# Queries loaded two groups at a time, two tokens on a partition, and put in order by copies of their transposes

## The chip, the cores and the metric

The kernel runs on one core of one Trainium2 chip. The metric is the device time of one execution in microseconds (us). One profiled execution gives the trace that is read here. In it, PE is the matrix engine (PEld its weight loads), DVE, ACT and POOL are the vector, scalar and GpSimd engines, and SP only issues transfers. "L224" is line 224 of the kernel as listed.

## The reference, cut to what matters

The input is four batches of 8 heads, 768 tokens and 64 features. Lightning attention works on blocks of 64 tokens, with a state that decays from block to block; its output, 512 wide for a token, goes through a mixture of depths, in which 128 tokens of each batch, those with the highest gate score, pass an expert of two matrices.

```
for b in range(768 // 64):
    intra = (q_b @ k_b.T * Dmask) @ v_b          # Dmask: lam ** (i - j), zero above the diagonal
    inter = (q_b * lam_pow) @ kv_state
    out[b] = intra + inter
    kv_state = lam_block * kv_state + (k_b * rev_pow).T @ v_b
x = out, heads side by side                      # (4, 768, 512)
scores = x @ w_gate
top = the 128 tokens of a batch with the highest scores
out[top] = x[top] + sigmoid(scores[top]) * (relu(x[top] @ w1) @ w2)
```

## The kernel before

**Groups.** A group is 128 tokens (two blocks) of one batch with all 8 heads, so there are 24 groups, six a batch (`NT`). The main loop runs over `g` from 0 to 23. Step g finishes group g, makes the scores of group g+1, and prepares group g+2: its transposes, decayed queries and state products. The order of all instructions on each engine is the order of the program; the kernel writes it out by hand. Each engine works through its instructions in that order, and an instruction that waits holds up those behind it.

**Loads.** `load(g)` fetches queries, keys and values of a group as three DMAs of 256 KB from the SP queue, each a tile of 128 partitions (tokens) by 8 heads by 64 features. One head of one token is contiguous in memory: 256 bytes, one packet. In `fetch_in` (L67) a load waits for the one three before it, except in a stretch in which the weights are loaded, so that about three are under way. The main loop asks for loads three to five groups ahead.

**Transposes.** Scores need queries and keys with features on the partitions. For groups under `SPLIT` (16), `transposes(g)` makes four PE transposes of queries (L219; each takes two heads, 128 x 128) into the PSUM tile `tq`, and ACT copies `tq` to its part of `qkT` in SBUF in one instruction (L224). Then come four of keys (L233) into `tk` and their copy (one copy, L238, up to group 7; two, L243, after that, because the keys' transposes then lie in the banks of the state products `pu`). From group 16 on `split_transposes` does it in another way (L257, with copies L263 to L265).

**What follows.** POOL multiplies keys and queries by their decay (`kd` L205, `qs` L270) and the states (`decayed` L318). PE makes the state products (`pu` L308), scores (L285), the part from states (L345) and the part from scores (L356); DVE masks the scores (`p` L292) and adds the states (L335, or L330). ACT copies outputs to `x_b` (L370, L372), from which DVE takes the gate scores (`xg` L395). A row of scores is turned by PE (`pb` L418), copied by ACT (`sc_row` L421), and compared by DVE (L424, L434).

**PSUM banks.** `tq`, `tk`, `tqk`, `pb`, `pk` and the expert's tiles share two PSUM banks in turn (`bank`); while the expert holds one (`hold=True`, tiles `ph` and `py`), all others take turns in the one left.

**Experts.** `plan(b)` spreads the expert of batch b over later steps. Work is put at a step with a key, and `in_order` runs what stands at one step by rising keys; the expert's 16 pieces have keys 10, 20, 30. `ranks` and `tokens` find the chosen tokens: PE counts in `pk` (L486), and DVE turns this into indices (`tok_f` L492, `tok` L495), with which POOL gathers rows (`fetch`, L509).

Of the kernel before, what the change touches and what calls it, by code (L numbers as in the profile page):

```python
# [8 lines left out]
FP32 = mybir.dt.float32  # L9
# [8 lines left out]
def kernel(  # L18
# [12 lines left out]
    nc = tc.nc  # L31

    B, H, S, D = q.shape
    HD = H * D
    F = moe_w1.shape[1]
    CAP = moe_capacity
    L = 128
    C = 64
    NT = S // L
    NHP = H // 2  # L40
# [5 lines left out]
    SPLIT = 2 * NT + 4  # L46
    FED = 2 * NT
    half = [slice(0, C), slice(C, 2 * C)]
    assert D == 64 and H % 2 == 0 and S % L == 0 and HD == 512 and F % 512 == 0
    assert 0 <= CAP < S  # L50

    const = ctx.enter_context(tc.tile_pool(name="const", bufs=1))
    ld = ctx.enter_context(tc.tile_pool(name="ld", bufs=7))
# [8 lines left out]
    loaded, issued = {}, []  # L62

    def fetch_in(out, in_):


        dma = nc.sync.dma_start(out=out, in_=in_)  # L67
        n, n_w1, n_w2 = len(issued), F // 256, NFC * HD // 512
        if 3 <= n < 3 * (NT + 3) + n_w1 or n >= 3 * (FED + 1) + n_w1 + n_w2:
            tc.add_manual_dep(  # L70
                dma.ins, issued[-3].ins.name,
                mybir.DependencyInfo(mybir.DependencyClass.Sync, mybir.DependencyReason.DATA),
                reason="loads under way",
            )
        issued.append(dma)

    def load(g):
        b, c = divmod(g, NT)
        rows = slice(c * L, (c + 1) * L)
        tiles = []  # L80
        for name, src in (("qn", q), ("kn", k), ("vn", v)):
            t = ld.tile([128, H, D], FP32, name=name)
            fetch_in(t[:], src[b, :, rows, :].rearrange("h p d -> p h d"))
            tiles.append(t)
        loaded[g] = tiles
# [14 lines left out]
    def load_weights(i):  # L100
# [13 lines left out]
    ident = const.tile([128, 128], FP32, name="ident")  # L114
# [10 lines left out]
        out=not_before[:], in_=not_before[:], compare_op=ALU.is_ge, fill=0.0,  # L125
# [58 lines left out]
    def bank(shape, name, hold=False):  # L184

        tag = next(t for t in banks if t not in held)
        banks.remove(tag)
        banks.append(tag)
        if hold:
            held.append(tag)  # L190
        return ps_m.tile(shape, FP32, name=name, tag=tag)
# [20 lines left out]
    def transposes(g):  # L212
        if g >= SPLIT:
            return split_transposes(g)

        W = NHP // 2
        tq = bank([128, NHP, L], "tq")
        for hp in range(NHP):
            nc.tensor.transpose(  # L219
                tq[:, hp, :], in_=loaded[g][0][:, 2 * hp : 2 * hp + 2, :], identity=ident[:]  # L220
            )
        qkT = att.tile([128, 2, 2, NHP, C], FP32, name="qkT")
        chunks = qkT[:].rearrange("p c n a i -> p n a c i")
        nc.scalar.copy(  # L224
            out=chunks[:, 0], in_=tq[:].rearrange("p a (c i) -> p a c i", c=2)
        )
        if g < SPARE + 2:
            both = bank([128, NHP, L], "tk")
            tk = [both[:, i * W : (i + 1) * W, :] for i in range(2)]
        else:  # L230
            tk = [u[:, NHP * D :].rearrange("p (a i) -> p a i", i=L) for u in us[g]]
        for hp in range(NHP):
            nc.tensor.transpose(  # L233
                tk[hp // W][:, hp % W, :], in_=loaded[g][1][:, 2 * hp : 2 * hp + 2, :],
                identity=ident[:],
            )
        if g < SPARE + 2:
            nc.scalar.copy(  # L238
                out=chunks[:, 1], in_=both[:].rearrange("p a (c i) -> p a c i", c=2)
            )  # L240
        else:
            for i in range(2):
                nc.scalar.copy(  # L243
                    out=chunks[:, 1, i * W : (i + 1) * W],
                    in_=tk[i].rearrange("p a (c i) -> p a c i", c=2),
                )
        qkTs[g] = qkT
# [342 lines left out]
    def put(step, key, piece):  # L590
        later.setdefault(step, []).append((key, piece))
# [5 lines left out]
    def plan(b):  # L597
# [3 lines left out]
        if last:  # L601

            def last_row():
                compare_older(NG - 1)
                row(NG - 1, us[NG][1])
                compare(NG - 1)
                ranks()

            put(s, 35, last_row)
            put(s, 85, tokens)  # L610
        else:

            if b > 0:
                ranked[s + 1] = ranks
                if s + 8 <= NG:
                    put(s + 2, 1, tokens)
                else:
                    early.setdefault(s + 2, []).append(tokens)
            else:
                put(s, 1, ranks)  # L620
                put(s, 2, tokens)
        for i in range(NGR):
# [12 lines left out]
            if first:  # L635
                put(s, 26, fetch)
                front[s + 1] = gate
            elif s + 8 <= NG:

                put(s + 2, 2, fetch)  # L640
                gates[s + 4] = gate
            else:
                early.setdefault(s + 2, []).append(fetch)
                gates[s + 3] = gate
# [192 lines left out]
```

## Time and profile before

| | |
|---|---|
| time, median of 3 runs | 186.22 us (184.71 to 186.49) |
| span of the profiled execution | 180.2 us |
| PE, DVE, POOL, ACT busy | 149.8, 111.5, 96.2, 68.9 us |
| packets moved, in all | 83381, of which 75665 under 512 bytes |
| query copy of L224, 128x512, 16 times | 585 ns (median) |
| a load of queries, issue to landing | 4.6 us (median) |

The span of a profiled execution is not the time of a run without the profiler: compare spans with spans and times with times. In the table of slices each digit is the busy share of a fortieth of the span, 4.5 us, in tenths. In the list of waits, "A <- B: 9.5, 7, 2.2" says that A's engine sat idle before A until B released it, 9.5 us in all, 7 times, at most 2.2 us. The chain is the work that ended last, followed back from the last instruction; asked for a stretch, it is followed back from the end of that stretch. "issue" is idle time for which the profile shows no releaser.

### The profile page before, as it was taken

How to read it: one execution, taken by the hardware profiler on the slowest of the kernel's cores; microseconds unless marked ns; L12 is line 12 of the kernel's file. 1: busy time of each engine (PE TensorE's matmuls, PEld its weight loads, DVE VectorE, ACT ScalarE, POOL GpSimd, SP SyncE). 2: the span in 40 equal slices, each digit the busy share in tenths (PEclk: the TensorE clock that was granted, in tenths of full speed). 3: DMA queues.
4: the chain of work that ended last, by engine and by line, in shares of the span. 5: the costliest groups of instructions: out<-in, count | busy, mean ns of one | idle time of the engine just before them, and what ended most of it. 6: DMA issues, size and time to landing. Idle time of an engine off the chain costs nothing.

```text
span 180.2 us, 8244 instructions
## 1 busy us (share of the span) xinstructions
PE 149.8 (83%) x3586; PEld 119.5 (66%) x3586; DVE 111.5 (62%) x378; ACT 68.9 (38%) x178; POOL 96.2 (53%) x100
## 2 busy tenths in 40 slices
PE   0799777776497999999977989989999997989980
PEld 0568666665386999776655668977666896459620
DVE  4814788899844445768996583589865779330010
ACT  2214555562144344644552552563343641011100
POOL 4358666945074665569786967867574600220002
PEclk9999999999859999999999999999999999999997
DMA  4999798999999998987999999989112131011001
GB/s 97 205 226 219 195 261 221 235 276 307 289 248 272 208 275 180 199 181 174 262 242 290 225 253 245 256 215 238 62 64 62 62 125 50 7 55 58 0 0 58
DMA packets 83381, 31.99 MB, mean 177 GB/s; under 512 B 75665, under 2 KB 79761, under 8 KB 83346
## 3 DMA queue, kind: packets, MB, share of 16 engines
q1 hardware_dynamic: 82560, 29.37, 67.8%
q0 software_dynamic: 640, 2.10, 3.4%
q8 instruction: 28, 0.46, 1.1%
q14 instruction: 7, 0.06, 0.1%
q10 hardware_dynamic: 146, 0.01, 0.0%
HBM read 24.12 MB, written 7.34 MB: 175 GB/s over the span
## 4 chain that ended last, share of the span: by engine, by line
PE 55%; issue 16%; DVE 14%; POOL 6%; DMA 4%; ACT 2%; POOLq 1%; ACTq 0%
PE py L561 10%; PE ph L547 9%; PE pu L308 6%; PE po L356 6%; PE po L345 5%; PE po L285 5%; DVE cmp L434 5%; PE tq L219 5%; POOL qs L270 2%; POOL decayed L318 2%; DMA qn<-in_q_dram 2%; DVE state L335 2%; DMA out_dram<-y,tok 2%; PE tqk L257 2%; DVE p L292 2%
## 5 line engine op out<-in xcount | busy, mean ns | idle before, releaser
L270 POOL TENSOR_TENSOR qs<-qkT,qpow 128x512 f32<-128x512 f32 x24 | 33.0, 1377 | 16.9 <-ACT qkT L224 9.5
L318 POOL TENSOR_TENSOR decayed<-state,decay 128x256 f32<-128x256 f32 x34 | 28.9, 849 | 23.1 <-DVE state L335 10.8
L547 PE MATMUL ph<-xsT,w_sb 128*128 128x128 f32 x256 | 31.1, 278 | 0.7 <-ACT xsT L523 0.7
L547 PEld LDWEIGHTS ph<-xsT,w_sb 128*128 128x128 f32 x256 | 29.5, 192 | 2.5 <-ACT qkT L264 1.2
L561 PE MATMUL py<-w_sb,hs 128*128 128x512 f32 x64 | 30.0, 602 | 0.1
L434 DVE TENSOR_SCALAR_CACHE_REDUCE cmp<-sc_row,sc 128x128 bf16<-128x128 f32 (+4 forms) x65 | 29.8, 503 | 0.0
L205 POOL TENSOR_TENSOR kd<-kn,kpow 128x512 f32<-128x512 f32 x24 | 25.8, 1074 | 4.9 <-DMA kn<-in_k_dram 4.9
L335 DVE TENSOR_TENSOR state<-pu,decayed 128x256 f32<-128x256 f32 x34 | 14.3, 422 | 16.3 <-ACT qkT L243 4.5
L395 DVE CUSTOM_DVE_ANT_0 xg<-x_b,wg_b 128x512 f32<-128x512 f32 x24 | 23.3, 969 | 0.0
L308 PE MATMUL pu<-vn,kd 64*64 64x64 f32 x704 | 19.3, 234 | 2.7 <-issue 1.2
L285 PE MATMUL po<-qkT 64*64 64x64 f32 x768 | 17.6, 227 | 4.1 <-issue 3.4
L292 DVE TENSOR_TENSOR p<-po,mask 128x512 f32<-128x512 f32 x24 | 16.5, 689 | 6.3 <-PE po L345 6.2
L308 PEld LDWEIGHTS pu<-vn,kd 64*64 64x64 f32 x704 | 16.4, 145 | 5.4 <-POOL kd L205 2.6
L356 PEld LDWEIGHTS po<-vn,p 64*64 64x64 f32 x768 | 14.3, 138 | 7.6 <-issue 5.7
L285 PEld LDWEIGHTS po<-qkT 64*64 64x64 f32 x768 | 15.1, 142 | 4.9 <-issue 3.8
L356 PE MATMUL po<-vn,p 64*64 64x64 f32 x768 | 17.8, 229 | 0.7 <-issue 0.7
L224 ACT COPY qkT<-tq 128x512 f32<-128x512 f32 x16 | 9.3, 584 | 23.2 <-PE tq L219 23.2
L561 PEld LDWEIGHTS py<-w_sb,hs 128*128 128x128 f32 x64 | 11.3, 191 | 10.0 <-issue 9.6
L372 ACT COPY x_b<-po 64x256 f32<-64x256 f32 x48 | 17.6, 366 | 0.6
L345 PE MATMUL po<-state,qs 64*64 64x64 f32 x704 | 17.2, 225 | 0.3 <-POOL qs L270 0.3
L219 PE MATMUL tq<-ident,qn 128*128 128x128 f32 x64 | 12.2, 322 | 5.1 <-DMA qn<-in_q_dram 5.1
L421 ACT COPY sc_row<-pb 128x128 f32<-128x128 f32 x22 | 5.9, 267 | 25.7 <-PE pb L418 25.6
(77 smaller groups left out, 182.7 us busy)
## 6 DMA issues: line engine op xcount, KB each, us to landing
qn<-in_q_dram SPq DMA_DIRECT2D x24, 256.0 KB, 4.6
kn<-in_k_dram SPq DMA_DIRECT2D x24, 256.0 KB, 4.4
vn<-in_v_dram SPq DMA_DIRECT2D x24, 256.0 KB, 4.8
out_dram<-x_b SPq DMA_DIRECT2D x18, 256.0 KB, 4.0
w_sb<-in_moe_w_dram SPq DMA_DIRECT2D x4, 512.0 KB, 5.7
w_sb<-in_moe_w_dram SPq DMA_DIRECT2D x8, 256.0 KB, 4.5
out_dram<-x_b SPq DMA_DIRECT2D x2, 768.0 KB, 6.4
xs<-out_dram,tok POOLq DMA_INDIRECT x4, 4.2
```

What stands on the lines that cost most here:

```text
L205: nc.gpsimd.tensor_tensor(out=kd[:], in0=loaded[g][1][:], in1=kpow[:].rearrange("p a b -> p (a b)").unsqueeze(2).broadcast_to([128, H, D]) ...
L219: nc.tensor.transpose(tq[:, hp, :], in_=loaded[g][0][:, 2 * hp : 2 * hp + 2, :], identity=ident[:])
L270: nc.gpsimd.tensor_tensor(out=qs[:].rearrange("p c a i -> p c (a i)"), in0=qkTs[g][:, :, 0].rearrange("p c a i -> p c (a i)"), in1=qpow[:] ...
L285: nc.tensor.matmul(po[half[c], hh, 1, hp, :], lhsT=qkT[half[hh], c, 1, hp, :], rhs=qkT[half[hh], c, 0, hp, :], start=True, stop=True, skip ...
L308: nc.tensor.matmul(us[g][c][half[hh], hp * D : (hp + 1) * D], lhsT=kd[half[c], h, :], rhs=vn[half[c], h, :], start=True, stop=True, skip_g ...
L318: nc.gpsimd.tensor_tensor(out=t[:], in0=states[n][:], in1=decay[:], op=ALU.mult)
L345: nc.tensor.matmul(pos[g][half[hh ^ c], hh, 0, hp, :], lhsT=qs[half[hh], c, hp, :], rhs=states[n][half[hh], hp, :], start=(hp == 0), stop= ...
L356: nc.tensor.matmul(pos[g][half[hh ^ c], hh, 0, hp, :], lhsT=p[half[c], hh, hp, :], rhs=vn[half[c], 2 * hp + hh, :], start=(hp == 0 and (2 ...
L395: nc.vector.tensor_tensor_reduce(out=xg[:], in0=x_bs[b][:, t].rearrange("p a b e -> p (a b e)"), in1=wg_b[:], scale=1.0, scalar=0.0, op0=A ...
L434: nc.vector.tensor_scalar(out=cmp[:, : cols.stop - cols.start], in0=rows_[b][:, cols], scalar1=scs[b][:, t : t + 1], scalar2=None, op0=op, ...
L547: nc.tensor.matmul(ph[:, fc % 4, :], lhsT=w1_sb[:, dc, fc * 128 : (fc + 1) * 128], rhs=keep["xsT"][:, dc, :], start=(dc == 0), stop=(dc == ...
L561: nc.tensor.matmul(py[:], lhsT=keep["hs"][:, fc, :], rhs=w2_sb[:, fc, :], start=(fc == 0), stop=(fc == NFC - 1),)
```

## The change

For groups 0 to 15 the queries of two neighbouring groups, 256 tokens, are loaded in one DMA of 512 KB. A partition takes two tokens that follow each other, so that 512 bytes of a head are contiguous, one packet. Group g even has partitions 0 to 63, and g odd 64 to 127. The packets of these queries are half as many. Eight transposes of 64 partitions by 128 (the two tokens of a head) take the place of four of 128 by 128; in their results even tokens have features on partitions 0 to 63, and odd ones on 64 to 127. Four copies, one for each parity of the head and parity of the token, put this in order: each reads a half of `tq`'s partitions and writes every second column of a half of `qkT`'s. Two of them stay on their half of the partitions, and two cross to the other. The layout of `qkT` is as it was, so all that follows is unchanged.

The limits at which loads stop and begin to wait for the third before them are counted anew (`loads_of`), since there are fewer loads. Query tiles get buffers of their own: four of two groups, and five of one. And the tokens and the gather of an expert that is neither the first nor a late one (that of batch 1, at step 14) are put after the first piece of the expert at that step instead of before it (keys 15 and 16 instead of 1 and 2).

```diff
     def load(g):
...
-        for name, src in (("qn", q), ("kn", k), ("vn", v)):
+        if g >= SPLIT:
+            qn = ld.tile([128, H, D], FP32, name="qn", bufs=5)
+            fetch_in(qn[:], q[b, :, rows, :].rearrange("h p d -> p h d"))
+        elif g % 2 == 0:
+            qn = ld.tile([128, H, 2, D], FP32, name="q2", bufs=4)
+            fetch_in(
+                qn[:].rearrange("p h s d -> p h (s d)"),
+                q[b, :, c * L : (c + 2) * L, :].rearrange("h (p s) d -> p h (s d)", s=2),
+            )
+        else:
+            qn = loaded[g - 1][0]
+        tiles.append(qn)
+        for name, src in (("kn", k), ("vn", v)):
...
-        tq = bank([128, NHP, L], "tq")
-        for hp in range(NHP):
+        tq = bank([128, H, L // 2], "tq")
+        own = half[g % 2]
+        for h in range(H):
             nc.tensor.transpose(
-                tq[:, hp, :], in_=loaded[g][0][:, 2 * hp : 2 * hp + 2, :], identity=ident[:]
+                tq[:, h, :], in_=loaded[g][0][own, h, :, :].rearrange("p s d -> p (s d)"),
+                identity=ident[own, own],
             )
...
-        nc.scalar.copy(
-            out=chunks[:, 0], in_=tq[:].rearrange("p a (c i) -> p a c i", c=2)
-        )
+        for hh in range(2):
+            for s in range(2):
+                nc.scalar.copy(
+                    out=chunks[half[hh], 0, :, :, s::2],
+                    in_=tq[half[s], hh::2].rearrange("p a (c i) -> p a c i", c=2),
+                )
...
-                    put(s + 2, 1, tokens)
+                    put(s + 2, 15, tokens)
...
-                put(s + 2, 2, fetch)
+                put(s + 2, 16, fetch)
```

## The prediction

> **What bounds the kernel now.** I read the busy table first, then the waits, then the chain through the stages in which queries of groups 0 to 15 are transposed (5 to 92 us), then its timeline.
>
> ```profile
> PE 149.8 (83%) x3586; PEld 119.5 (66%) x3586; DVE 111.5 (62%) x378; ACT 68.9 (38%) x178; POOL 96.2 (53%) x100
> ...
> DMA  4999798999999998987999999989112131011001
> ...
> q8 instruction: 28, 0.46, 1.1%
> ```
>
> The DMA engines are nine tenths busy up to 126 us, so a change that halves the packets of the queries looks like a cure. But a busy queue costs only where an engine waits for it, and the waits tell who does:
>
> ```profile
> POOL qs L270 <- ACT qkT L224: 9.5, 7, 2.2
> ...
> PE tq L219 <- DMA qn<-in_q_dram: 5.1, 1, 5.1
> ...
> POOL kd L205 <- DMA kn<-in_k_dram: 4.9, 2, 3.1
> DVE state L335 <- ACT qkT L243: 4.5, 3, 1.7
> ...
> PE po L285 <- issue: 3.4, 3, 1.5
> ```
>
> (Columns: total us, times, longest.) Loads are waited for at the start (5.1, and 3.1 of the 4.9) and once at 106.87 us (1.80 us, keys of group 19, whose loads the change leaves alone). Behind the copies of transposes stand POOL (9.5 us) and DVE (4.5 us). ScalarE is 38% busy over all, but in the middle its first copy is a link of the chain, row by row (start, us):
>
> ```profile
> 80.48 0.59 ACT qkT L224
> 81.08 0.07 issue
> 81.14 0.79 POOL qs L270
> 81.93 0.44 issue
> 82.37 1.18 POOL decayed L318
> 83.55 1.01 POOL kd L205
> 84.56 0.04 issue
> 84.61 0.69 PE pu L308 x32
> 85.30 0.60 PE tq L219 x4
> 85.96 0.04 issue
> 86.00 0.59 ACT qkT L224
> ```
>
> One turn takes 86.00 - 80.48 = 5.52 us, and nothing in it waits for a load. What lengthens the query copy lengthens the turn.
>
> **What the Trainium skill says.** "ScalarE: Activation LUTs", What ACT_TABLE_LOAD costs: an instruction with immediate operands takes 186 ns plus 0.833 ns an element of the free side; neighbours overlap by about 93 ns. The trace agrees roughly: 512 elements 585 ns, 256 elements 366 to 383 ns; two L243 copies end 0.66 us after the first began (overlap 0.1), but two L372 copies, which cross halves of the partitions, take 0.74 (no overlap). So 64 partitions are no cheaper than 128. "DMA: Bandwidth & Descriptors", Why small descriptors are slow: a packet costs its 32-byte beats plus about 3 cycles, so 11 cycles for 256 bytes and 19 for 512; a pair of groups would then take 19/22 of its former engine time, not half. No run here shows 512-byte packets. "Runtime: NRT & Kernel Launch", Instruction fetch mechanics: instructions come by DMA in blocks of 256. The trace agrees: PE and PEld have 7172 records, 28 such blocks, as many as the packets of q8; and PE stops inside one run of matmuls, with no semaphore in it, at 39.97 us (0.81), 44.85 (1.48) and 93.17 (1.15).
>
> **Copies on ScalarE (the largest part).** Per group, one copy of 128x512 (0.585 us) becomes four of 64 partitions by 256 elements. Low: they overlap as L243's, 3 x 0.28 + 0.37 = 1.21. High: as L372's, 4 x 0.37 = 1.48. Two of the four cross halves, so I take 1.39: +0.8 us. I assume that the stride of two elements in the output costs nothing; no row shows one. The four queue behind each other, then the key copy behind them, so keys, too, are ready 0.8 us later. In sum 16 x 0.8 = 13 us more ScalarE work.
>
> **Transposes.** 4 of 128x128 become 8 of 64 rows. L219's weight loads begin 94 ns apart, so four take 0.39 us; L257 does the same 64-row form, each half of the rows at 62 ns intervals, so eight on one half take 0.50. I take +0.1 us (high end: 8 x 94 ns, +0.36). With the copies d = 0.9 us (low 0.7, high 1.25) from the first transpose to queries ready.
>
> **What d costs, step by step.**
> Start: q0 lands at 4.95, then k0, v0, q1 each about 1.15 us later, 228 GB/s. The pair now stands ahead of k0. Bounds on its extra time: 0 (a 512-byte packet costs as a 256-byte one) and 19/11 of 1.15 less 1.15 = 0.84. On the chain behind it stand k0's transposes, its copy at 7.32 and the scores at 7.96; the key copy also waits some tenths for the four. I take +1.0 (0.3 to 1.3).
> Queries 2 to 6 (15 to 37 us): the turn is 4.43 us, closed by DVE (xg, then pb at 21.82). The query copy begins 3.1 us after pb and pb takes the bank it reads: 3.1 + 1.39 + 0.06 = 4.55 us a turn, 0.1 more, five times: +0.5 (0 to 1.0).
> Query 7 (38.16): pb already waits 0.35 us for this copy: +0.9. Queries 8 and 9 (49.91 and 56.30): PE's state products start 0.1 us after the first key copy ends (50.87, 57.24): +0.9 each.
> Queries 10 and 11 (63.86, 70.02): PE is filled by ph. POOL's kd ends 0.7 and 0.2 us before PE needs it, so 0.2 + 0.7 = +0.9.
> Queries 12, 13, 14 (74.96 to 86.59): the chain shown above: 3 x 0.9 = +2.7. Query 15 (90.98): its key copy releases DVE's state at 92.06, and rank, hit, xg and the state that PE waits for at 95.78 follow on DVE without a gap: +0.8.
> Sum: 1.0 + 0.5 + 0.9 + 1.8 + 0.9 + 2.7 + 0.8 = +8.6 us. Later groups use the old form, and I see no slack that takes the shift back.
>
> **Tokens and fetch after the first piece (step 14).** PE's pk waits 0.78 us at 97.89 for ScalarE to empty tqk, and two py matmuls stand behind it. Now py (0.97 us) runs first. DVE's tok_f cannot be before 98.41, when xg ends, so the gather is not later; pb can start at 98.6 instead of 98.98: -0.4 us (0 to -0.8).
>
> **Relief of the DMA engines.** 16 groups lose 512 packets each, 8192 of 83381. No chain piece between 8 and 100 us is a load, so nothing comes directly. The gaps inside runs of matmuls sum to 5.0 us (0.81, 1.48, 1.15, 0.37, 0.30, 0.91), and a less crowded queue may shorten those before 90 us. Bounds 0 and -5.0, and -1.8 if the wait at 106.87 went too; I take a third of the gaps, -1.7. The wait of the SP queue for the load three back now lets a 512 KB load count as one; loads are asked three to five groups ahead, so this is hidden by that lead. Addresses and the choice of tiles cost nothing on the chip.
>
> **The sum.** 8.6 - 0.4 - 1.7 = +6.5, so 186.2 + 6.5 = 192.7 us. Low end, every copy overlapped, start at 0.3 and most gaps gone: 0.3 + 7 x 0.7 + 0.8 - 0.8 - 3.5 = +1.7, 187.9. High end, d of 1.25 and no relief: 1.3 + 1.0 + 7 x 1.25 + 1.3 = +12.4, 198.6.
>
> **Rivals.**
> Faster: the crowded DMA engines hold more than the waits name. If all the gaps (5.0), the load wait (1.8) and 0.4 at the tokens go, and the copies hide in ScalarE's idle 62%, up to 7 us could be had; with the three chained turns lengthened (+2.7) it is 186.2 - 7.2 + 2.7 = 181.7. For it speaks the row of nines; against it, that 23.2 us of ScalarE's idle time is spent waiting for exactly these transposes, so the idle time isn't where the copies fall.
> A draw: copies overlap (d = 0.7), only queries 7, 8, 9, 12, 13, 14 are on the path (+4.2), start even, relief -3.5, tokens -0.4: 186.5.
> Worse: PE idles longer at 44 to 52 us, where its granted clock is already 0.73 from 51 to 58. Another 3 us at that clock, with matmuls at up to double (pu's 32 took 1.26 us there, 0.65 elsewhere), adds 2 to 3 us: 192.7 + 2.5 = 195.2.
>
> **How the numbers follow.** Forecast (192.7, with its two ends) 0.62, worse 0.13, draw 0.12, faster 0.13. I forecast 192.7. The range: the forecast's ends and the worse case up to 196.5, the draw inside, and down to 185.5, which leaves out most of the faster case and the far top. Faster by over 1% 0.13, within 1% 0.12, slower by over 1% 0.75.
>
> **What would show it.** The step right: four copies on tq with a mean of 366 ns or so; POOL's wait for L224's successor up from 9.5 us by 6 or more; the turn from 80 us at 6.3 to 6.5 us instead of 5.52; pk behind py with no wait of 0.78. The gaps inside runs of matmuls before 90 us tell the relief. It is wrong if the copies take under 0.25 us each or overlap wholly, if the gaps shrink by more than the copies add, or if the turn at 80 us stays at 5.5 us.

## The result, and the profile after

The changed kernel takes 201.0 us (median of 4 runs, 198.55 to 203.05), the kernel before in the same comparison 185.5 us (183.93 to 186.49). The ratio is 1.080, with a 95% interval of 1.066 to 1.095. The change makes the kernel 15.5 us slower by the medians, more than twice what was forecast. One of the four runs of the changed kernel (203.05 us) was in a slower state and is left out of the ratio, which stands for 14.8 us.

The page of the changed kernel comes first: the busy table, two rows of the slices (granted clock and DMA), the packets and the queue of instructions.

```profile
PE 158.4 (81%) x3650; PEld 125.8 (64%) x3650; DVE 108.6 (55%) x378; ACT 84.9 (43%) x226; POOL 95.3 (48%) x100
...
PEclk9999999999658699999999999998899999999997
DMA  3999569699999997979968949891013221011001
...
DMA packets 75062, 32.00 MB, mean 163 GB/s; under 512 B 59153, under 2 KB 71441, under 8 KB 75026
...
q8 instruction: 29, 0.48, 1.1%
```

The packets fell by 8319 (83381 before); 8192 of these are the queries', as forecast. The DMA row has lost several of its nines. ACT gained 16.0 us of work (68.9 before) where the forecast had 13. None of the relief shows as time.

From the list of waits (total us, times, longest), with new line numbers:

```profile
POOL qs L295 <- ACT qkT L248: 16.8, 8, 3.4
...
DVE state L360 <- ACT qkT L268: 10.0, 5, 2.9
PEld pb L443 <- ACT qkT L248: 10.0, 9, 1.4
...
PE tq L240 <- DMA q<-in_q_dram: 6.3, 1, 6.3
...
POOL kd L223 <- DMA kn<-in_k_dram: 4.3, 1, 4.3
```

POOL's wait for the query copy rose by 7.3 us (9.5 before), DVE's wait for the key copy behind it by 5.5 (4.5 before), and PE's weights for `pb` now wait for the query copy nine times. The first load, which is twice as large, is waited for 1.2 us longer; the 4.3 us for keys belong to the start too. No later load stands in the list with a wait of over 1 us. The chain names one, a load of values that lands at 113.56 us, in the step from group 15 to 16, in which the changed kernel loses 0.3 us (table below).

The chain, in the stretch that the forecast read (start, us):

```profile
84.84 0.39 ACT qkT L248
85.24 0.39 ACT qkT L248
85.64 0.38 ACT qkT L248
86.03 0.39 ACT qkT L248
86.49 0.83 POOL qs L295
87.72 1.18 POOL decayed L343
88.91 1.01 POOL kd L223
89.96 0.69 PE pu L333 x32
90.65 0.66 PE tq L240 x8
91.41 0.39 ACT qkT L248
```

It is the same ring of work as before. One turn takes 91.41 - 84.84 = 6.57 us instead of 5.52. The four copies begin 0.40 us apart, none beside another, and take 86.03 + 0.39 - 84.84 = 1.58 us where the single copy took 0.59.

To see where the 15.5 us arise, I take from the timeline of DVE the start of `p`, the masking of scores, for each group. The first column is the kernel before (us), the others are differences to it in the changed kernel and in four of the experiments below (e9: pair loads alone; e2: four copies alone, each on its half of the partitions; e17: four copies alone, as the change has them; e15: pair loads and those copies).

```
group  before   e9 loads  e2 straight  e17 crossing  e15 loads+crossing  changed
  0     15.14     +1.09       +0.24        +0.20           +1.37          +1.90
  1     19.24     +0.05       +0.14        -0.29           +0.76          +2.21
  6     41.87     +1.65       +0.70        +1.46           +2.98          +4.57
  8     54.86     +1.81       +1.21        +2.53           +3.59          +5.75
  9     62.77     +1.81       +2.58        +5.76           +6.86          +8.22
 11     74.43     +2.66       +3.05        +6.58           +7.69          +9.23
 15     95.91     +3.43       +6.45       +10.96          +12.07         +13.99
 16    101.50     +3.12       +8.37       +12.89          +12.75         +14.32
 19    119.91     +3.87       +8.30       +12.64          +12.49         +13.80
 23    143.88     +3.87       +8.28       +12.65          +12.50         +16.81
```

Each column is one execution, and that of the kernel before was a short one: its span is 180.2 us, while 138 timed runs of the same kernel average 182.7. So the columns end some 2.5 us too high on that account; what is read from them is where a difference begins. From group 1 to 15 the changed kernel loses 0.84 us a group in the mean. A jump of 2.5 to 3.4 us at group 9 stands in every kernel that has the four crossing copies, but also in the changed kernel with one copy (e6 below, +2.15).

After group 15 no query copy of the new form is left, and yet the changed kernel loses 3.0 us more between groups 19 and 23. Of these 2.3 come at group 20, where 16 matmuls of the expert (`ph`) take 3.45 us from 135.93 us on (1.95 before), a little behind a gap of 0.93 us that has no releaser. PE's clock was at a half just there (a window of the changed kernel; the columns are us, busy us of PE, PEld, DVE, ACT and POOL with counts, granted clock, DMA share, GB/s):

```profile
135.00:140.00 5.00, 4.38 (x20) 3.75 (x19) 3.52 (x17) 1.72 (x4) 3.78 (x4) 0.66 0.01 3
```

In the kernel before, the clock is whole from 55 us until PE has ended.

### The profile page after: what moved, and what is told of

Same layout as the page of the kernel before. It is cut to its first block, busy times and chain, and to the rows that moved or that the text cites. A ratio compares the mean times of both kernels' runs of the same rounds, so it can differ in the third digit from the quotient of the medians.

```text
span 196.5 us, 8422 instructions
## 1 busy us (share of the span) xinstructions
PE 158.4 (81%) x3650; PEld 125.8 (64%) x3650; DVE 108.6 (55%) x378; ACT 84.9 (43%) x226; POOL 95.3 (48%) x100
## 3 DMA queue, kind: packets, MB, share of 16 engines
q1 hardware_dynamic: 74240, 29.37, 60.2%
## 4 chain that ended last, share of the span: by engine, by line
PE 52%; issue 13%; ACT 10%; POOL 8%; DVE 7%; DMA 6%; SPq 1%; POOLq 1%; ACTq 0%
PE ph L572 9%; ACT qkT L248 9%; PE py L586 7%; PE pu L333 7%; PE tq L240 6%; PE po L381 5%; PE po L370 5%; PE po L310 5%; POOL qs L295 3%; DVE cmp L459 3%; POOL decayed L343 3%; DMA q<-in_q_dram 3%; DMA vn<-in_v_dram 2%; PE pb L443 2%; PE tqk L282 2%
## 5 line engine op out<-in xcount | busy, mean ns | idle before, releaser
L343 POOL TENSOR_TENSOR decayed<-state,decay 128x256 f32<-128x256 f32 x34 | 28.4, 835 | 25.2 <-DVE state L360 11.3
L248 ACT COPY qkT<-tq 64x256 f32<-64x256 f32 x64 | 24.6, 384 | 25.8 <-PE tq L240 25.2
L572 PE MATMUL ph<-xsT,w_sb 128*128 128x128 f32 x256 | 33.8, 292 | 1.0 <-ACT xsT L548 0.7
L572 PEld LDWEIGHTS ph<-xsT,w_sb 128*128 128x128 f32 x256 | 32.1, 206 | 2.0 <-ACT xsT L548 1.3
L360 DVE TENSOR_TENSOR state<-pu,decayed 128x256 f32<-128x256 f32 x34 | 14.3, 422 | 25.4 <-ACT qkT L268 10.0
L333 PE MATMUL pu<-vn,kd 64*64 64x64 f32 x704 | 19.7, 238 | 7.5 <-issue 2.8
L420 DVE CUSTOM_DVE_ANT_0 xg<-x_b,wg_b 128x512 f32<-128x512 f32 x24 | 20.1, 839 | 0.0
L370 PE MATMUL po<-state,qs 64*64 64x64 f32 x704 | 17.7, 230 | 1.1 <-POOL qs L295 0.6
L240 PE MATMUL tq<-ident,q 64*128 64x64 f32 x128 | 12.9, 251 | 6.3 <-DMA q<-in_q_dram 6.3
L370 PEld LDWEIGHTS po<-state,qs 64*64 64x64 f32 x704 | 15.3, 145 | 1.9 <-issue 1.0
```

The lines of the kernel that those rows point to most:

```text
L240: nc.tensor.transpose(tq[:, h, :], in_=loaded[g][0][own, h, :, :].rearrange("p s d -> p (s d)"), identity=ident[own, own],)
L248: nc.scalar.copy(out=chunks[half[hh], 0, :, :, s::2], in_=tq[half[s], hh::2].rearrange("p a (c i) -> p a c i", c=2),)
L333: nc.tensor.matmul(us[g][c][half[hh], hp * D : (hp + 1) * D], lhsT=kd[half[c], h, :], rhs=vn[half[c], h, :], start=True, stop=True, skip_g ...
L343: nc.gpsimd.tensor_tensor(out=t[:], in0=states[n][:], in1=decay[:], op=ALU.mult)
L370: nc.tensor.matmul(pos[g][half[hh ^ c], hh, 0, hp, :], lhsT=qs[half[hh], c, hp, :], rhs=states[n][half[hh], hp, :], start=(hp == 0), stop= ...
L572: nc.tensor.matmul(ph[:, fc % 4, :], lhsT=w1_sb[:, dc, fc * 128 : (fc + 1) * 128], rhs=keep["xsT"][:, dc, :], start=(dc == 0), stop=(dc == ...
```

## The experiments

All ratios are to the kernel before, run on the same chip, with 95% intervals.

### The parts by themselves: tokens, copies, pair loads

The first theory was the forecast's: the copies bring the loss. Its rivals were the loads and the start.

Tokens behind the first piece, and nothing else (e1):

```diff
-                    put(s + 2, 1, tokens)
+                    put(s + 2, 15, tokens)
...
-                put(s + 2, 2, fetch)
+                put(s + 2, 16, fetch)
```

> The kernel before with the tokens and the gather of batch 1 put after the first piece of their step, and nothing else changed. Theory 'copies' (the four query copies make the loss): 185.1 us, 0 to 0.8 less than before. Theory 'tokens' (the later gather starts a new wait downstream): 187 or more.

Measured: 183.25 us, 0.998 (0.995 to 1.001). The gain of 0.4 us that was forecast can't be told from nothing.

Four copies of 64 partitions in the kernel before, each staying on its half of the partitions (e2):

```diff
-        nc.scalar.copy(
-            out=chunks[:, 0], in_=tq[:].rearrange("p a (c i) -> p a c i", c=2)
-        )
+        for hh in range(2):
+            for s in range(2):
+                nc.scalar.copy(
+                    out=chunks[half[hh], 0, :, :, s::2],
+                    in_=tq[half[hh]].rearrange("p a (c i) -> p a c i", c=2)[:, :, :, s::2],
+                )
```

> The kernel before, in which only the query copy of groups 0 to 15 is made as four copies of 64 partitions by 256 elements with a stride of two on both sides; loads and transposes as before, and no copy crosses halves of the partitions. Theory 'copies': 10 to 13 us slower than before (195.5 to 198.5), each copy near 0.38 us and 0.40 us from start to start, the turn at 80 us near 6.5 us. Theory 'loads' (the larger loads and their start make most of the loss): at most 4 us slower (189.5). If only crossing copies keep from overlapping, a turn is 0.3 us shorter than in the changed kernel and the loss some 3 us less.

Measured: 189.92 us, 1.031 (1.023 to 1.039), 5.9 us more. That is less than half of the loss and fits neither theory. But the turn is 0.30 us shorter than in the changed kernel, which is what the expectation gave for the case that only crossing copies keep from overlapping:

```profile
78.43 0.66 ACT qkT L226 x2
...
79.10 0.67 ACT qkT L226 x2
...
84.70 0.66 ACT qkT L226 x2
```

Here two copies on one half of the partitions take 0.66 us. The third, on the other half, begins only when the second has ended (79.10), so four take 1.33; a turn is 84.70 - 78.43 = 6.27 us.

Pair loads in the kernel before, with four transposes of 128 rows and one copy (e9):

```diff
...
+            q2 = ld.tile([128, 2, H, D], FP32, name="q2", bufs=4)
+            fetch_in(
+                q2[:].rearrange("p s h d -> p (s h d)").rearrange("p (h e) -> p h e", h=H),
+                q[b, :, c * L : (c + 2) * L, :].rearrange("h (p s) d -> p h (s d)", s=2),
+            )
+            pairs[g + 1] = q2
+            tiles.append(q2[:, 0])
...
```

> The kernel before with the loads of the changed one (pairs of groups, 512 KB, 512-byte packets, their buffers), but with its own four transposes of 128x128 and single copy, and its own keys of the tokens; it leaves out putting the queries in their order, each group taking half of the heads of both groups. One copy in place of four left 8.2 us of loss. Theory 'loads': most of these come from here, 5 to 9 us over before (189 to 193). Theory 'transposes': under 3 us, the rest being the transposes of 64 rows.

The same, with groups 0 and 1 loaded singly (e10):

```diff
-        if g >= SPLIT:
+        if g >= SPLIT or g < 2:
```

> As the pair loads alone, but groups 0 and 1 loaded singly in packets of 256 bytes; it leaves out putting the queries of groups 2 to 15 in order. Theory 'start' (q of the first pair lands 1.24 us later, and the granted clock rises later with it): 3 us or more less than with the first pair, and within 2 us of before. Theory 'loads throughout': within 1.5 us of the pair loads alone.

Measured: 185.73 us, 1.003 (0.999 to 1.007), and 183.89 us, 1.007 (1.002 to 1.013). By the ratios, pair loads cost at most 0.7% (e9) or 1.3% (e10); by the medians e10 is 0.4% faster than before (184.68 in both comparisons), so nothing is told from this difference. What is shown is that halving the packets of the queries wins nothing that can be measured, and costs at most one to two microseconds. The later landing of the first pair is made good here: the table's column e9 starts 1.09 us late and is back at +0.05 one group later.

### The set without the copies, and an order restored by PE

The changed kernel with one 128x512 copy, so that the order of tokens is not restored (e6):

```diff
-        for hh in range(2):
-            for s in range(2):
-                nc.scalar.copy(
-                    out=chunks[half[hh], 0, :, :, s::2],
-                    in_=tq[half[s], hh::2].rearrange("p a (c i) -> p a c i", c=2),
-                )
+        nc.scalar.copy(
+            out=chunks[:, 0],
+            in_=tq[:].rearrange("p h i -> p (h i)").rearrange("p (a c i) -> p a c i", c=2, i=C),
+        )
```

> The changed kernel with a single copy of 128x512 in place of the four; it leaves out putting the tokens and heads in order, all other work is the same. Theory 'copies': the loss goes but for the start and the transposes, 186 to 189. Theory 'loads': 194 or more, since loads, buffers and transposes are those of the changed kernel.

Measured: 192.21 us, 1.046 (1.039 to 1.052). This lies between the two expectations. The copies are not all: 8.2 us stay without them, of which the loads make under one. What is left is the form of the transposes, eight of 64 rows (and the tokens, which e1 puts at nothing).

The changed kernel with PE restoring the order, 16 products of 64x64 that write every second column, and one copy (e3):

```diff
...
+        for hp in range(NHP):
+            for s in range(2):
+                for hh in range(2):
+                    nc.tensor.matmul(
+                        tq[half[hh], hp, s::2], lhsT=loaded[g][0][own, 2 * hp + hh, s, :],
+                        rhs=ident[own, own], start=True, stop=True, skip_group_check=True,
+                    )
...
```

> The changed kernel in which PE itself puts the tokens in order: sixteen products of 64x64 with the identity for a group, each written to every second column of its half of tq, and then one copy of 128x512 as before. Theory 'copies': as with one copy, 186 to 189; sixteen products on two quadrants take about 0.5 us, as the eight transposes do. Theory 'loads': 194 or more. If the relief of the DMA engines is worth what the change was made for, it ends below 185.5.

Measured: 201.15 us, 1.095 (1.086 to 1.104). No better, and not for the reason of the theory 'loads', in whose range it falls: the trace has 512 PE instructions for these 256 products, so an fp32 product takes two where a transpose takes one, and ACT's wait for them is 40.6 us (23.2 before the change).

### Which groups' transposes

The changed kernel with groups 0 and 1 in their old form (load, transposes, copy; e5):

```diff
-        if g >= SPLIT:
+        if g >= SPLIT or g < 2:
...
+        if g < 2:
+            tq = bank([128, NHP, L], "tq")
+            for hp in range(NHP):
+                nc.tensor.transpose(
+                    tq[:, hp, :], in_=loaded[g][0][:, 2 * hp : 2 * hp + 2, :], identity=ident[:]
+                )
...
```

> The changed kernel with groups 0 and 1 loaded, transposed and copied as before. Theory 'start': 4 us less than the changed kernel (197), since the landing (1.24), the copies of group 0 (0.5) and the later rise of the clock go. Theory 'loads throughout': 199 to 200, the 1.24 and 0.5 us alone.

Measured: 196.08 us, 1.064 (1.056 to 1.072). Two groups of sixteen are worth 1.6% of 185 us, 3 us (4.9 by the medians), near the theory 'start'; but the two intervals (1.066 to 1.095 for the change) overlap, so this is a hint and no more.

Three kernels without the copies (one copy, order not restored) choose by group between pair tiles with 64-row transposes ("half"), pair tiles with 128-row ones ("full"), and single loads:

```diff
+    def form(g):
+        return "single" if g >= SPLIT else "single" if g < 2 else "half"    # e11
+        return "single" if g >= SPLIT else "half" if g < 2 else "full"    # e13
+        return "single" if g >= SPLIT else "half" if g >= 8 else "full"    # e14
```

> The pair load, the eight transposes of 64 rows and one copy (order not restored), for groups 2 to 15; groups 0 and 1 are loaded singly and transposed in four of 128 rows, as before the change. The whole set without the four copies (all 16 groups) took 1.0455 of the kernel before, some 8.2 us more; the pair loads with 128-row transposes took 1.003. If the 64-row transposes cost by the first two groups (PE reaches its full rate later), this takes 1.00 to 1.015 (184 to 187.5 us). If they cost throughout, 1.03 or more (189.5 us or more).

> Pair loads for groups 0 to 15, one copy (order not restored); eight transposes of 64 rows for groups 0 and 1 alone, four of 128 rows for groups 2 to 15. If the cost lies in the first two groups, 1.02 to 1.045 (188 to 192 us); if it lies in all of them in turn, 1.00 to 1.015 (184.5 to 187 us).

> Pair loads for groups 0 to 15, one copy (order not restored); eight transposes of 64 rows for groups 8 to 15 alone, four of 128 rows for groups 0 to 7. If the 64-row transposes cost evenly throughout, half of the 8 us: 1.02 to 1.025 (188 to 189 us). If at the start alone, 1.00 to 1.01 (184.5 to 186 us). If by the clock and the expert's stages behind group 8, 1.03 or more (190 us or more).

Measured: e11 187.43 us, 1.018 (1.011 to 1.024); e13 186.84 us, 1.015 (1.011 to 1.020); e14 187.05 us, 1.011 (1.007 to 1.015). e11 lies between the expectations; e13 lies at the edge of the one for a cost in all groups in turn, and e14 at the edge of the one for a cost at the start alone, so neither theory holds as put. Against the same kernels with 128-row transposes: groups 2 to 15 cost 1.0176 - 1.0074 = 1.0% (0.9 either way), 1.9 us or 0.13 a group, near the 0.1 of the forecast. Groups 0 and 1 alone cost 1.0154 - 1.0029 = 1.25% (0.6 either way), 2.3 us. Together that is 4.2 us, but all sixteen at once cost 1.0455 - 1.0029 = 4.3%, 7.9 us. By the medians of the same runs the three are 1.5, 0.2 and 3.9%. So how the cost is shared between the first two groups and the rest isn't settled; that the parts don't add up to the whole holds either way.

A place where the first groups' cost could come from is the time at which PE begins to work at its full rate. In the first microseconds of all these traces, a run of matmuls takes about twice as long as the same run later (32 matmuls `pu` of the changed kernel 1.06 us of the chain at 12.79 us, and 0.47 at 21.39). The chain of the set without copies, and that of e13, at the transposes of group 2 (both were alike up to there):

```profile
17.35 1.05 PE tq L240 x8
```

```profile
17.34 0.59 PE tq L256 x4
```

In the first, PE is still at half its rate (eight transposes take 0.66 us later), and it stays so until 23.0 us; in e13 it is at the full rate. PE turned to it at 17.4 us before, 19.7 in the changed kernel, 14.3 with its first groups as before, 15.9 with the pair loads alone. The slices of granted clock don't show this; the durations do.

But these two kernels were alike up to that point, so what came before can't be why they differ there. And e1, which is the kernel before in all these groups, turned to the full rate about 3 us sooner than it (ten matmuls of the first state part, the kernel before and then e1):

```profile
13.98 0.80 PE L345 MATMUL po<-state,qs 64*64 64x64 f32 x10
```

```profile
14.01 0.52 PE L345 MATMUL po<-state,qs 64*64 64x64 f32 x10
```

So the same program gets its full rate at times that differ by 3 us from one execution to another, and single profiles can't tie this time to the form of the transposes.

### As many instructions, whole rows

The kernel before with eight products of 128 rows against half of the identity's columns (e12):

```diff
-            nc.tensor.transpose(
-                tq[:, hp, :], in_=loaded[g][0][:, 2 * hp : 2 * hp + 2, :], identity=ident[:]
-            )
+            for c in range(2):
+                nc.tensor.matmul(
+                    tq[:, hp, c * C : c * C + C], lhsT=loaded[g][0][:, 2 * hp : 2 * hp + 2, :],
+                    rhs=ident[:, half[c]], start=True, stop=True, skip_group_check=True,
+                )
```

> The kernel before with eight PE products for a group's queries in place of four transposes: the same 128 rows as weights, against one half of the identity's columns each, so that the result is the same, with as many PE instructions and as many moving columns as the change has, but with all rows of the array used. If the number of instructions (and their fetch) is what the eight transposes cost, 1.025 to 1.04 of before (188.5 to 191.5 us). If it is that they use half of the rows, 0.995 to 1.015 (183 to 187 us).

Measured: 211.33 us, 1.142 (1.132 to 1.152). Both expectations missed, and the run doesn't answer its question, since each product takes two instructions, as the tile's line shows:

```profile
L220 PE MATMUL tq<-ident,qn x256: 216/275/473, 5.1 to 115.9; 128*128 128x64 f32 x128
```

Its chain has 16 instructions in 1.93 us where four transposes took 0.60 at the full rate. The 1.33 us more appear undiminished in the steps of groups 12 to 15 (+1.35, +1.35, +1.33, +1.40 us in the start of `p`): what is put between the state products and the query copy is paid in full there.

### PE at work before the first load

If the late full rate is what the first groups cost, PE could be set to work earlier. In four kernels (w1: before; w2: changed; w3: e6; w4: e9), transposes of the identity, used by nobody, run from 1.43 us on, 12 in w1 (2.8 us) and 16 in those with pair loads (3.7 us):

```diff
+    warm = ps_o.tile([128, 2, 2, NHP, C], FP32, name="po")
+    warm = warm[:, 0].rearrange("p a b i -> p (a b i)")
+    for i in range(12):
+        nc.tensor.transpose(warm[:, :128], in_=ident[:], identity=ident[:])
     keys_decayed(0)
     transposes(0)
```

> The kernel before with 12 more transposes of the identity on PE, between 1.5 us and the landing of the first queries; their result is used by nobody. In the profile of before, PE's products take twice as long until 17.4 us. If PE's rate is set by how long it has been at work, it is full some 3.5 us earlier and 1.5 to 4 us of the run go: 0.98 to 0.99 of before (181.5 to 184 us). If the rate rises at a given time, whatever PE did, 0.995 to 1.005.

> The changed kernel with 16 transposes of the identity ahead of its first queries' transposes. The changed kernel took 1.080 of before, and 1.064 with groups 0 and 1 in their old form. If those 4.9 us are PE reaching its full rate later, they go, and more of the slow stretch with them: 1.04 to 1.055 (192 to 195 us). If they are waits for the larger load and the four copies at the start, what goes is what goes from the kernel before: 1.06 to 1.07 (196 to 198 us).

> Pair loads and 64-row transposes for all 16 groups, one copy (order not restored), with 16 transposes of the identity ahead. Without these it took 1.0455, and 1.0176 when groups 0 and 1 had their old form. If the difference is PE's rate at the start: 1.00 to 1.02 (185 to 188.5 us). If not: 1.03 or more (190.5 us or more).

> Pair loads with 128-row transposes and one copy (order not restored), with 16 transposes of the identity ahead. Without these it took 1.003. If PE's rate is set by how long it has been at work: 0.98 to 0.995 (181.5 to 184 us), and the difference from the same with 64-row transposes is what those cost once the start is equal, 2 to 4 us. If not: 0.995 to 1.01.

Measured: before 185.59 us, 1.005 (1.000 to 1.010); changed 200.82 us, 1.090 (1.086 to 1.095); one copy 193.39 us, 1.035 (1.028 to 1.043); pair loads 187.90 us, 1.010 (1.003 to 1.017). None gained; w1, w3 and w4 fall at or in the ranges for a rate that this work doesn't bring, and w2 misses both of its ranges. The full rate began at 16.1, 17.7, 22.0 and 17.3 us, against 17.4, 19.7, 23.0 and 15.9 without this work: three are 1 to 2 us sooner and one 1.4 later, all within the 3 us by which one program differs from execution to execution. So the theory as I had put it, full some 3.5 us earlier, falls for work of this kind. The extra work was transposes alone; other products weren't tried. That the 64-row set is late in both of its profiles (23.0 and 22.0) stays unexplained.

### The whole change with 128-row transposes

Pair loads, four copies, tokens, but four transposes of 128 rows of the pair tile, in all groups (e15) and in groups 2 to 15 (e16):

```diff
+            for hp in range(NHP):
+                if form(g) == "full":
+                    in_ = loaded[g][0][:, NHP * (g % 2) + hp, :, :].rearrange("p s d -> p (s d)")
...
+                nc.tensor.transpose(tq[:, hp, :], in_=in_, identity=ident[:])
```

> The changed kernel with four transposes of 128 rows of the pair tile in place of the eight of 64 rows, and all the rest as changed: pair loads, four copies, tokens (the transposed values are of other heads and tokens, so the order isn't restored). If the 64-row transposes cost 6 to 8 us here too: 1.03 to 1.045 (190 to 193 us), which is the copies' 1.031 and the pair loads' few tenths of a per cent. If it is the larger load and the four copies that hurt each other: 1.06 or more (195.5 us or more).

> The same, but with the eight transposes of 64 rows in groups 0 and 1, four of 128 rows in groups 2 to 15. If the 64-row transposes cost in the first two groups alone: as the changed kernel less 1 to 3 us, 1.06 to 1.075 (195.5 to 198 us). If they cost in all in turn: within 2 us of the kernel with none, 1.03 to 1.055 (190 to 194.5 us).

Measured: e15 195.86 us, 1.060 (1.054 to 1.066); e16 197.38 us against 184.6 (no interval; 194.11 to 199.33). So within the change the 64-row transposes cost 2.0% (about 3.7 us, with the intervals of both ratios some 3 us either way); e16 scatters too much to say in which groups. In their profiles the changed kernel stands 1.45 us behind e15 at group 1, 1.92 at group 15 and 4.31 at the end. So little of it arises in groups 2 to 15, and more than half after group 19, where both kernels transpose alike and the changed one alone has a lowered clock (0.66 from 135 to 140 us). And the pair loads with the copies cost 11.1 us, not 5.9 + 0.6. Either they hurt each other, or these copies aren't those of e2.

### Copies that cross

The kernel before, single loads, with the four copies exactly as the change has them (e17):

```diff
-        nc.scalar.copy(
-            out=chunks[:, 0], in_=tq[:].rearrange("p a (c i) -> p a c i", c=2)
-        )
+        tq = tq[:].rearrange("p a (b i) -> p (a b) i", b=2)
+        for hh in range(2):
+            for s in range(2):
+                nc.scalar.copy(
+                    out=chunks[half[hh], 0, :, :, s::2],
+                    in_=tq[half[s], hh::2].rearrange("p a (c i) -> p a c i", c=2),
+                )
```

> The kernel before (single loads, four transposes of 128 rows, tokens as before) with the four copies in the order and with the halves of the partitions that the change gives them, so that every second one crosses from one half to the other (the order isn't restored by it). With four copies that stay on their half, in pairs, it took 1.031 of before; four took 1.32 us. If the crossing is what makes the copies dearer: four take 1.57 us, 0.25 more, which lies on the chain of 10 to 14 groups, 3 to 4 us: 1.045 to 1.06 (192.5 to 195.5 us). If the larger load at the start and the copies together make the 11.2 us: 1.03 to 1.04 (189.5 to 191.5 us).

Measured: 194.07 us, 1.057 (1.050 to 1.065), 10.5 us more, as expected for copies that cross, and the same as e15 within their intervals. So the halves between which the copies go make the difference to e2, and the loads (with the tokens' new place) add nothing that can be measured in the time. Its chain:

```profile
88.48 0.39 ACT qkT L227
88.88 0.39 ACT qkT L227
89.27 0.38 ACT qkT L227
89.67 0.39 ACT qkT L227
90.13 0.91 POOL qs L274
```

A copy takes 384 ns in the median as against 382 in e2. It isn't longer, but it begins only when the one before has ended: the order straight, crossing, crossing, straight leaves no two neighbours that read and write the same halves. Four take 1.58 us instead of 1.33, and the turn goes from 6.27 to 94.98 - 88.48 = 6.50 us. Whether it is the crossing, or any change of half between neighbours, isn't separated: in e2 the second and third copy both stay on their half, but on different ones, and don't overlap either.

In the table, e17 loses another 2 us to e2 in one step, from group 8 to 9 (+3.23 against +1.37 us). A lowered clock stands at this place. The windows of e17, and then of the kernel before (columns as above):

```profile
50.00:55.00 5.00, 3.69 (x68) 3.32 (x72) 1.01 (x4) 2.16 (x6) 3.08 (x3) 0.50 0.98 228
55.00:60.00 5.00, 4.70 (x98) 4.34 (x91) 3.31 (x12) 2.45 (x7) 1.05 (x2) 0.58 1.16 302
60.00:65.00 5.00, 3.63 (x46) 3.52 (x47) 1.08 (x4) 1.50 (x5) 3.34 (x3) 0.76 1.00 207
```

```profile
50.00:55.00 5.00, 4.78 (x134) 4.29 (x133) 2.08 (x8) 2.16 (x6) 3.48 (x4) 0.52 1.07 247
55.00:60.00 5.00, 4.02 (x61) 3.68 (x60) 2.56 (x9) 1.81 (x5) 2.65 (x4) 1.00 0.98 282
60.00:65.00 5.00, 5.00 (x156) 4.76 (x155) 1.82 (x7) 2.50 (x7) 2.11 (x3) 1.00 0.95 216
```

PE's clock falls to a half between 45 and 50 us in both; before, it is whole again by 55 us, in e17 not until 65 to 70. And in e17 and e2 it falls once more, where before it stays whole: to 0.70 and 0.62 from 105 to 115 us in e17, to 0.73 and 0.59 from 100 to 110 us in e2. (So it does from 96 us on in e1 and e10, which have no such copies.) One profile could be chance, but every timed run comes with its span and mean granted clock, and span x (1 - clock) is the clock time lost in a run: 5.7 us in the mean of 138 runs of the kernel before (in its profile over 2 us of this lie at the end, after PE has ended); 5.3 with the pair loads; 7.9 with the straight copies and 7.9 in the set with one copy; 10.7 with the crossing copies, 10.0 in e15 and 10.5 in the changed kernel. In the six runs of e17 the mean clock was 0.937 to 0.955, against 0.969 in the mean of before, so this isn't one bad execution. The loss was 13.3 us in e12, which only lengthened PE's work. So a slower kernel lost more clock in most of these, but not in step with its time: 4.6 us in e13 (1.015), 14.4 in w2 (1.090). What makes PE lose it, and how much of it is paid in time, wasn't separated.

No version is measurably faster than the kernel before.

## Why the prediction was wrong

The direction and the mechanism were right, the size was not: +6.5 us was forecast, +15.5 measured by the medians and +14.8 by the ratio, and even the high end (+12.4) lies under both. The step that failed most is the price of the four copies: 1.39 us was taken, at most 1.48, and 1.58 measured, and so 6.7 us for their turns where the copies alone cost 10.5 (e17). The second is the relief of -1.7 us, of which nothing came. The third is the row of the 64-row transposes, +0.1 a group: within the change they cost about 3.7 us (changed kernel against e15, some 3 either way), and by which way isn't known. Pair loads and tokens together make about 0.6 (e15 against e17). These three differences are steps of one row of kernels, so that they add up to 14.8 is no check.

**Copies: mechanism shown, price too small.** The signs named in advance are there: four copies of 384 ns, POOL's wait up by 7.3 us, a turn of 6.57 us, idle ScalarE no help. With the copies alone (0.8 a group) the forecast's steps sum to about 6.7 us; the crossing copies cost 10.5. The forecast took 1.39 us for four, between full overlap and none, because two of the four cross. It read rightly that a crossing copy doesn't overlap, but not that, in this order, the straight ones then have no neighbour to overlap with; and its own high end was built from 0.37 us, not the 0.384 + 0.01 measured. That is 0.2 us a turn, and the steps of groups 13 to 15 grew by 1.0 instead of 0.8. In queries 2 to 6 the effect is larger: there the turn is closed by the copies. The 3.1 us from `pb` to the copies were read rightly; with 1.58 in place of 1.39 the turn became 4.73 us in the changed kernel (27.33 to 32.06) instead of the 4.55 forecast, and the five steps cost 1.75 us in e17's column (group 1 to 6) and not 0.5. With the measured 1.58 us the forecast's own sum for the copies gives about 9.6 us (1.55 for queries 2 to 6, 1.0 for each of 7, 8, 9, 12, 13 and 14, 1.1 for 10 and 11, 0.9 for 15), inside the interval of e17 (9.1 to 11.9). With the 1.33 us of e2 it gives about 6.1, and 5.9 were measured. So the path was worked out rightly, and the price put on it was not.

**The clock: a rival that was partly there.** The forecast had a lower clock of PE as a rival of its own, +2.5 us with a chance of 0.13. It goes with these copies in every kernel that has them: 8.8 to 11.2 us of clock lost a run without the extra work, against 5.7 before. In the profiles it stands at the jump at group 9 and, in the changed kernel, at the 2.3 us of group 20. But a jump of 2.15 us at group 9 stands in e6 as well, and the copies' 10.5 us come out of the turns within the interval of e17, so what the clock adds to the time isn't separated.

**Relief of the DMA engines: a term with nothing behind it.** -1.7 us were taken for gaps inside runs of matmuls. The pair loads alone are worth 1.003 (0.999 to 1.007): nothing came. The gaps longer than 0.25 us, counted alike, sum to 6.0 us before and 7.1 after (before 90 us, which was to tell the relief, to 3.3 and 5.2), and lie between 3.8 and 10.7 in the experiments without an order that follows the packets. The price of a packet was fair: "DMA: Bandwidth & Descriptors" in the Trainium skill (Why small descriptors are slow) counts 11 cycles for 256 bytes, from which the forecast's estimate for 512 bytes was 19, 1.7 times as much; the trace's median packets take 18 and 27 ns, 1.5 times, and the queue's time fell by only 3.9 us of 16 engines (67.8% of 180.2 to 60.2% of 196.5, 122.2 to 118.3 us).

**Transposes: right in the row, wrong in the sum.** Eight take 0.71 us against 0.66 (0.66 and 0.60 in the chain), and in groups 2 to 15 with one copy they cost 0.13 us each (0.1 either way), near the forecast. But all sixteen together cost 7.9 us with one copy and about 3.7 within the change, and the sum has nothing of that size. Their cost in groups 0 and 1 is 2.3 us by the ratios and under half a microsecond by the medians. The cause stays open: the time of PE's full rate differs by 3 us between executions of one program, and the clock that the changed kernel loses at 135 us comes after the last of these transposes.

**Start.** The pair landed 1.24 us later than the single load (at most 0.84 was allowed), and group 0 was masked 1.90 us late. The forecast took it as paid in full (+1.0). Alone it is made good one group later (e9). With the copies it is not: e15 stands 1.05 us behind e17 at group 1 and 1.11 at group 15, and draws level only at group 16.

**Tokens.** As forecast or nothing: 0.998 alone. In the changed kernel the wait of 0.78 us of `pk` is gone, and `pb` starts 2.84 us after `pu` instead of 3.20, 0.36 sooner, as forecast. At group 16 the kernels with the old place lose 1.9 us (e2, e17) and those with the new one 0.7 and 0.3 (e15, changed). That looks like a larger gain beside longer copies, but e2 and e17 have their second stretch of lowered clock just there and the changed kernel has none, so the place isn't shown to be the cause.

The draw and the faster rival fell with e9 and e10: the row of nines in the DMA slices held nothing that fewer packets of queries could win.

## What to carry to other kernels

Ask what waits for a resource before relieving it: here the DMA engines were nine tenths busy, halving the queries' packets won nothing, and the copies that bought the relief stood in a ring in which every tenth of a microsecond was paid once a turn. When one instruction is split into several, price the split by neighbours of the same kind in the same order, since overlap belongs to pairs of instructions and not to one. And before a difference of a microsecond or two between two profiles is explained, look at the granted clock in that stretch and at how far two executions of one program differ.

## What the runs showed of the hardware

- On ScalarE, two neighbouring copies of 64x256 on one half of the partitions take 0.66 us, overlapping by 0.1; in the order straight, crossing, crossing, straight they begin 0.40 us apart and don't overlap, and two straight ones on different halves don't overlap either (e2). "ScalarE: Activation LUTs" (What ACT_TABLE_LOAD costs) gives an overlap of about 93 ns for neighbours in general; the measurement restricts it. A stride of two elements in the output (in e2 in the input too) costs little: 382 to 384 ns against 366 for the plain 64x256 copy.
- An fp32 product on PE takes two instructions with a weight load each (256 for 128 products in e12, 512 for 256 in e3), a transpose one; eight 64x128 transposes take about as long as four of 128x128 (0.66 and 0.60 us in the chain).
- PE works at about half its rate until 14 to 23 us into the run, which the granted clock doesn't show. The same program reached the full rate at 17.4 and at about 14.3 us in two executions (before and e1), and 2.8 to 3.7 us of transposes ahead of the first load moved it by no more than that.
- The granted clock falls to a half for some microseconds in the middle of a run, and in most of the slower kernels more often or longer: from 48 to 55 us in the profile of before; from 45 to 60, 62 to 66 and 107 to 114 us in that of e17.
